# A convolution, layer norm and feed-forward kernel on one core: products moved from VectorE to GpSimd in the head, ScalarE for the first statistics, a finer tail, a new order

## The chip, the cores and the metric

The kernel runs on one core of a Trainium2 chip. The metric is the device time of one execution in microseconds; the time before is the median of three runs, 844.35 us. One execution was also taken with the hardware profiler: it took 843.82 us, and its span, from the first to the last instruction, is 842.0 us. TensorE (PE), VectorE (DVE), ScalarE (ACT) and GpSimd (POOL) work through queues of their own in order; SyncE (SP) issues most of the DMA transfers, and GpSimd issues those that add onto data in place.

## The reference

For x of shape (8, 4224, 192) and weights of shape (8, 4224, 8, 7), both float32:

```python
w = softmax(weight_gen, over the 7 taps)               # per token and head
x_pad = 6 zero tokens ahead of x                       # per batch
out[b, s, h, :] = sum_k w[b, s, h, k] * x_pad[b, s + k, h, :]     # 8 heads of 24 channels
xn = (out - mean) / sqrt(var + 1e-6) * g_ln
result = out + maximum(xn @ w_ch1, 0) @ w_ch2          # 192 -> 768 -> 192
```

The weights of the feed-forward part are given as float64.

## The kernel before

The 33,792 tokens lie on 128 partitions, 264 columns of 192 channels each; a column is one token per partition. Work goes by parts of 4, 4, then 8 and then 12 columns (`PARTS`, L22), cut into chunks of 2, 4 or 6 columns, and by groups of 4 columns (`NT`) for the matmuls.

The softmax (`softmax`, L451) makes log-weights for pieces of 4, 8 and then 12 columns: a maximum on VectorE, a subtraction on GpSimd, an exponential on ScalarE, the sum on VectorE (for two early pieces on TensorE), a logarithm on ScalarE and a second subtraction, `less`, on GpSimd. For each chunk `conv` (L492) lets ScalarE write the exponentials `wn` (key `expw`) into PSUM, and VectorE multiplies x by them: taps 1 and 2 (key `c0`), 3 and 4 (`c1`), 0 (`c2`) and 5 and 6 (`c3`), each pair into a product buffer `pr`, of which there are five. For the first three chunks (`PMUL = 3`) `c3` is GpSimd's, from a copy of the exponentials in SBUF (key `keep`). The seven products of the first three chunks are summed by TensorE (`z0` to `z3`, matmuls with the identity), whose result ScalarE copies back. In later chunks two DMA additions issued by GpSimd (`d0`, `d1`) and four additions on GpSimd (`a0` to `a3`) do it.

`norm` (L599) takes mean and variance. For parts that start below column 8 (`STATS = 8`) VectorE does it with `bn_stats` (key `stats`), two columns at a time; later ScalarE does it in two passes per column with an accumulator (`sums`, `squares`). `rstd` on ScalarE and `newton` on VectorE follow, then ScalarE normalizes (`xh`). For the first two groups TensorE transposes (`tp`) and ScalarE and VectorE split the result into two float16 halves (`thi`, `tlo`). From the third group on the split is `hi` on ScalarE and `lo` on GpSimd and the transpose is a DMA that SyncE issues (`turn`), kept apart from the DMA additions: each waits until the last one of the other kind has landed.

For each group TensorE then computes three units of the first product into the two `ph` buffers (`unit`, L780, 36 matmul pairs); ScalarE applies the relu into a float16 half (`relu`, L796) and VectorE computes the rest (`hlo`, L798), which frees `ph`. Two half passes `p0` and `p1` (L832) make the second product in the one `po` buffer, and VectorE adds it to the tokens (`f`, L884), which frees `po`; SyncE stores them. The last group's second product is made by `output` (L853): four tiles in pairs of two in one bank, one addition and one store for each pair.

Ahead of all this `weights` (L992) turns the float64 weights into scaled float16 halves on ScalarE and VectorE (keys that begin with `w_`); TensorE makes the low halves with scaled identities (`w_l`, `w_l2`), ScalarE copies them (`w_lc`, `w_lc2`).

The order of everything is written out by hand: `PLACE` (L39) gives each operation a place, operations are emitted in the order of their places, each into its engine's queue, and buffers are assigned in the same order:

```python
out = sorted(self.ops, key=lambda o: o.place)
...
b.slot = min(range(len(tenant[b.pool])), key=lambda i: freed(tenant[b.pool][i]))
```

Of the kernel before, what the change touches and what calls it, by code (L numbers as in the profile page):

```python
# [26 lines left out]
PMUL = 3  # L27
STATS = 8
# [11 lines left out]
    'wload': (0, 1, 15, 26, 98, 102, 176, 495, 321, 482, 657, 761, 837, 1034, 613, 1145, 1282, 1182, 951, 1438,  # L40
        1515, 1614, 1730,),
    'load': (2, 3, 5, 7, 9, 22, 43, 95, 105, 145, 143, 174, 92, 244, 288, 208, 297, 414, 325, 484, 497, 660,
        569, 626, 644, 719, 851, 815, 920, 942, 918, 1001, 1066, 1240, 1236, 1303, 1205, 1365, 1353, 1467, 1476,
        1619, 1541, 1592, 1669, 1749, 1853, 1832, 1814, 1980, 2003, 1949,),
    'w_load': (45, 13, 20,),
    'w_gain': (40, 38, 29,),
    'w_load2': (32,),
    'w_as': (88,),
    'w_ap': (90,),
    'w_av': (96, 99,),  # L50
    'w_an': (107,),
    'w_cs': (53,),
    'w_cp': (52,),
    'w_cv': (58, 60,),
    'w_cn': (80,),
    'w_s1': (113, 118,),
    'w_d': (150, 124,),
    'w_h': (127, 123,),
    'w_l': (155, 126,),
    'w_lc': (166, 130,),  # L60
    'w_m': (169, 172, 135, 133,),
    'w_c2s': (73, 103, 120,),
    'w_c2p': (71, 94, 125,),
    'w_c2v': (76, 79, 108, 110, 134, 138,),
    'w_c2n': (83, 116, 142,),
    'w_s2': (148, 156, 185,),
    'w_d2': (178,),
    'w_h2': (175, 164, 183,),
    'w_l2': (184, 181, 189,),
    'w_lc2': (200, 202, 194,),  # L70
    'max': (4, 11, 54, 64, 188, 281, 355, 559, 594, 537, 769, 881, 907, 1073, 1096, 1211, 1320, 1225, 1430,
        1502, 1679, 1770, 1960,),
    'sub': (6, 16, 59, 81, 193, 378, 448, 565, 599, 679, 779, 887, 972, 1091, 1124, 1261, 1400, 1415, 1513,
        1598, 1759, 1811, 2007,),
    'exp': (8, 21, 63, 111, 215, 382, 467, 592, 637, 709, 795, 903, 1023, 1105, 1148, 1276, 1412, 1459, 1581,
        1645, 1822, 1849, 2023,),
    'sum': (10, 25, 234, 390, 492, 601, 645, 721, 834, 946, 1032, 1138, 1178, 1279, 1435, 1511, 1605, 1676,
        1835, 1860, 2034,),
    'log': (12, 28, 86, 152, 249, 409, 498, 604, 658, 765, 858, 969, 1036, 1160, 1251, 1341, 1458, 1524, 1608,
        1699, 1856, 1869, 2060,),  # L80
    'less': (14, 31, 87, 160, 276, 421, 510, 606, 691, 771, 883, 987, 1058, 1193, 1257, 1344, 1478, 1559, 1650,
        1742, 1859, 1937, 2093,),
    'expw': (17, 30, 35, 56, 97, 139, 151, 199, 235, 266, 327, 356, 329, 434, 473, 516, 540, 623, 656, 703, 722,
        783, 820, 910, 960, 996, 1017, 1080, 1111, 1210, 1203, 1280, 1359, 1372, 1402, 1503, 1494, 1594, 1564,
        1678, 1721, 1775, 1796, 1888, 1944, 1972, 2058, 2145, 2102, 2104,),
    'keep': (18, 39, 65,),
# [16 lines left out]
    'copy': (50, 69, 119,),  # L103
    'stats': (61, 74, 144, 141,),
    'rstd': (77, 147, 209, 279, 354, 426, 502, 585, 693, 802, 895, 1002, 1102, 1201, 1307, 1420, 1501, 1623,
        1713, 1817, 1926, 2018, 2119, 2214, 2280, 2338,),
    'newton': (91, 153, 219, 285, 359, 432, 507, 591, 696, 804, 901, 1003, 1106, 1204, 1309, 1433, 1510, 1627,
# [10 lines left out]
    'thi': (136, 180,),  # L118
    'tlo': (159, 186,),
# [19 lines left out]
    'sums': (131, 168, 191, 187, 222, 242, 268, 258, 323, 310, 338, 334, 380, 399, 413, 411, 478, 457, 486, 490,  # L139
# [149 lines left out]
def kernel(  # L289
# [309 lines left out]
    def norm(pa):  # L599
# [3 lines left out]
        def row(i):  # L603
            if S0 < STATS:
                i = {1: 3, 2: 4}[i]
            return at(s4)[:, i, :n]
# [538 lines left out]
```

## Time and profile before

| | us |
|---|---|
| median of 3 runs | 844.35 (843.34 to 845.62) |
| profiled execution | 843.82 |
| span of it | 842.0 |
| PE busy | 821.4 (98%) |
| DVE busy | 736.5 (87%) |
| POOL busy | 701.6 (83%) |
| ACT busy | 683.8 (81%) |

The busy times are sums over the whole span. In the page's 40 slices of 21 us PE has 6, 8 and 8 tenths in the first three and 7 in the last, and 9 or more in between; DVE, ACT and POOL are at 9 tenths or near it until late and thin out in the last quarter. So the engines' shares of the whole say little about the first 60 us, which have limits of their own and are read by stretches.

### The profile page before, as it was taken

What the parts mean: (1) busy time and instruction counts of PE and PEld (TensorE: products, weight loads), DVE (VectorE), ACT (ScalarE), POOL (GpSimd) and SP (SyncE); (2) the same over time, 40 slices, a digit from 0 to 9 for tenths busy, and PEclk for the clock granted to TensorE, in tenths of its full rate; (3) what the DMA queues carried; (4) which work ended last, traced back from release to release, by engine and by line L of the source; (5) the groups of instructions that cost most, each with busy time, mean ns of one, the idle gap of its engine ahead of it and who ended that gap; (6) DMA issues with size and microseconds to landing.
All of it is one profiled execution on the core that took longest, in us unless ns stands there. A gap on an engine that the chain in (4) does not pass through costs nothing.

```text
span 842.0 us, 37407 instructions
## 1 busy us (share of the span) xinstructions
PE 821.4 (98%) x16724; PEld 811.3 (96%) x16724; DVE 736.5 (87%) x685; ACT 683.8 (81%) x1774; POOL 701.6 (83%) x402
## 2 busy tenths in 40 slices
PE   6889999999999999999999999999999999999997
PEld 5669999999999999999999999999999999999997
DVE  7999999999999999999999999999989896745332
ACT  3899998898998899898888979988888878776431
POOL 4999999999999999999999999899798879624000
PEclk9889999999999999999999999999999999999999
DMA  9997997989999997889878997777877766352432
GB/s 228 206 211 153 221 162 170 204 160 205 193 195 191 199 215 167 178 186 215 190 153 202 188 217 174 164 185 163 180 153 162 165 145 129 78 116 68 80 65 58
DMA packets 133887, 140.88 MB, mean 167 GB/s; under 512 B 104294, under 2 KB 106222, under 8 KB 133726
## 3 DMA queue, kind: packets, MB, share of 16 engines
q1 hardware_dynamic: 120190, 88.16, 45.9%
q0 software_dynamic: 13536, 50.34, 30.8%
q8 instruction: 130, 2.13, 1.0%
q14 instruction: 31, 0.25, 0.1%
HBM read 36.43 MB, written 25.95 MB: 74 GB/s over the span
## 4 chain that ended last, share of the span: by engine, by line
PE 82%; DVE 11%; issue 2%; POOL 2%; ACT 1%; DMA 1%; SPq 1%; DVEq 0%; POOLq 0%; ACTq 0%
PE po L832 41%; PE ph L780 40%; DVE pr L535 6%; DVE hlo L798 2%; DVE y L535 1%; POOL y L538 1%; DMA x<-in_x_dram 1%; PE ph L861 1%; DVE y L884 1%; POOL pr L541 1%; ACT hh L796 0%; DVE mx L466 0%; ACT junk L611 0%; DVE sm L482 0%; DVE s L628 0%
## 5 line engine op out<-in xcount | busy, mean ns | idle before, releaser
L538 POOL TENSOR_TENSOR y<-y,pr 128x1152 f32<-128x1152 f32 (+1 forms) x188 | 488.3, 2625 | 13.0 <-DVE y L535 4.3
L780 PE MATMUL ph<-xT,c_w 64*128 64x256 f16 x7128 | 412.9, 269 | 1.9 <-DVE hlo L798 1.3
L780 PEld LDWEIGHTS <-c_w 64*128 64x128 f16 x7128 | 386.2, 94 | 3.1 <-issue 2.9
L832 PE MATMUL po<-c_w2h,hh 64*128 64x192 f16 x3120 | 388.0, 243 | 1.1 <-DVE y L884 1.1
L832 PE MATMUL po<-c_w2l,hh 64*128 64x192 f16 x3120 | 388.0, 243 | 0.0
L832 PE MATMUL po<-c_w2h,hlo 64*128 64x192 f16 x3120 | 388.0, 243 | 0.0
L535 DVE TENSOR_TENSOR pr<-x,wn 128x2304 f32<-128x2304 f32 (+2 forms) x147 | 333.2, 2276 | 4.3 <-POOL y L538 2.5
L832 PEld LDWEIGHTS <-hh 64*128 64x128 f16 x6240 | 309.7, 94 | 1.4 <-issue 1.3
L798 DVE SCALAR_TENSOR_TENSOR hlo<-ph,hh 128x1024 f16<-128x1024 f32 x198 | 239.4, 1217 | 73.1 <-ACT hh L796 72.6
L796 ACT ACTIVATE hh<-ph 128x1024 f16<-128x1024 f32 x198 | 200.2, 1014 | 84.8 <-PE ph L780 80.6
L832 PEld LDWEIGHTS <-hlo 64*128 64x128 f16 x3120 | 177.6, 94 | 0.0
L758 POOL TENSOR_TENSOR hl<-xh,hl 128x768 f16<-128x768 f32 x64 | 114.7, 1828 | 49.1 <-ACT hl L756 48.3
L686 ACT ACTIVATE xh<-y,s 128x192 f32<-128x192 f32 x264 | 125.8, 536 | 17.2 <-DVE s L674 12.1
L616 ACT ACTIVATE junk<-y,s 128x192 f32<-128x192 f32 x256 | 115.8, 452 | 7.9 <-PE po L832 1.8
L541 POOL DMA_DIRECT2D pr<-pr x94 | 93.2, 1054 | 26.6 <-DVE pr L535 22.1
L611 ACT ACTIVATE junk<-y 128x192 f32<-128x192 f32 x256 | 92.1, 360 | 12.5 <-PE po L832 4.1
L884 DVE SCALAR_TENSOR_TENSOR y<-po,c_fs,y 128x768 f32<-128x768 f32 (+1 forms) x83 | 67.9, 835 | 7.4 <-PE po L832 7.2
L535 DVE TENSOR_TENSOR y<-x,wn 128x1152 f32<-128x1152 f32 (+2 forms) x50 | 59.9, 1199 | 0.0
L756 ACT ACTIVATE hl<-xh 128x768 f16<-128x768 f32 x64 | 53.4, 836 | 1.6 <-PE po L832 0.7
L611 ACT ACTIVATION_READ_ACCUMULATOR junk<-y 128x1 f32 x256 | 48.1, 188 | 0.0
L616 ACT ACTIVATION_READ_ACCUMULATOR junk<-y,s 128x1 f32 x256 | 47.9, 187 | 0.0
L486 POOL TENSOR_TENSOR e<-e,sm 128x672 f32<-128x672 f32 (+2 forms) x23 | 37.8, 1645 | 6.6 <-ACT sm L484 6.6
(86 smaller groups left out, 308.3 us busy)
## 6 DMA issues: line engine op xcount, KB each, us to landing
pr<-pr POOLq DMA_DIRECT2D x68, 576.0 KB, 6.1
x<-in_x_dram SPq DMA_DIRECT2D x34, 576.0 KB, 6.0
out_dram<-y SPq DMA_DIRECT2D x34, 576.0 KB, 4.9
pr<-pr POOLq DMA_DIRECT2D x26, 384.0 KB, 5.0
w<-in_weight_gen_dram SPq DMA_DIRECT2D x21, 336.0 KB, 5.1
x<-in_x_dram SPq DMA_DIRECT2D x14, 384.0 KB, 6.2
out_dram<-y SPq DMA_DIRECT2D x13, 384.0 KB, 5.2
x<-in_moe_w_ch_dram SPq DMA_DIRECT2D x1, 1152.0 KB, 11.3
```

Source lines behind the costliest of these rows:

```text
L535: E.tensor_tensor(out=ov, in0=xv, in1=wv, op=ALU.mult)
L538: Q.tensor_tensor(out=flat(0), in0=flat(0), in1=flat(k), op=ALU.add)
L541: return Q.dma_start(flat(to), flat(k), accum_op=ALU.add, max_dma_last_dim=CHUNK * D * 4)
L611: A.activation(junk, at(y)[:, j, :], AF.Identity, scale=-SQ / D, accum_out=at(s4)[:, 3, t : t + 1])
L616: A.activation(junk, at(y)[:, j, :], AF.Square, scale=SQ, bias=at(s4)[:, 3, t : t + 1], accum_out=at(s4)[:, 0, t : t + 1])
L686: A.activation(paired(xh, t), at(y)[:, i, :].rearrange("p (c q) -> p c q", q=P // 2), AF.Identity, bias=row(2 if quick else 3)[:, g + t : ...
L758: lambda xh=xh, hl=hl: Q.tensor_tensor(out=halves(hl, True), in0=pairs(xh), in1=halves(hl, False), op=ALU.subtract),
L780: T_.matmul(ph[:, r, v * 2 * P : (v + 1) * 2 * P], W["w1"][rows, WB[r][c], w, f : f + P], xv[rows, a, c, :, :], start=(v == 0 and k == 0), ...
L796: lambda: A.activation(at(hh)[:, us, :], at(ph), AF.Relu), [ph], [(hh, u)])
L798: lambda: V.scalar_tensor_tensor(out=at(hlo)[:, us, :], in0=at(ph), scalar=0.0, in1=at(hh)[:, us, :], op0=ALU.max, op1=ALU.subtract),
L832: made.append(T_.matmul(at(po)[:, z, e * D : (e + 1) * D], token(b, 2 * z + e, j)[rows], W[w][rows, j, :], start=(ph == 0 and e == 0 and k ...
L884: V.scalar_tensor_tensor(out=ysl, in0=at(po)[:, zs[0] : zs[-1] + 1, : 2 * D], scalar=W["fs"][:, 0:1], in1=ysl, op0=ALU.mult, op1=ALU.add)
```

## The change

`PMUL` becomes 4, and a new constant `PTWO` names column 2. GpSimd thereby makes `c3` of columns 8 to 11 and, for the chunk of columns 2 and 3, `c1` besides `c3`; the chunk of columns 8 to 11 gets a `keep` copy of its exponentials for that. `STATS` becomes a tuple with the one start 4: the statistics of columns 0 to 3 go from VectorE's `bn_stats` to ScalarE's two passes. The last four tiles go through a new function `last`: each tile into a bank of its own and with an addition of its own; columns 0 and 1 are stored together, 2 and 3 each by itself. The place list is new up to about place 480; after that each engine's order is as before, until the last tiles.

```diff
-PMUL = 3
-STATS = 8
+PMUL = 4
+STATS = (4,)
+PTWO = (2,)
...
-            if c < PMUL and i == 3:
+            if c < PMUL and (i == 3 or i == 1 and t0 in PTWO):
                 op("Pool", q_ns(2 * nd), (f"c{i}", t0), lambda k=k: mul(k, 2, Q), [*xr, (e, "w", c)], w)
...
-            if S0 < STATS:
+            if S0 in STATS:
...
-        quick = S0 < STATS
+        quick = S0 in STATS
...
+    def last(gp, t, s):
+        e = t % 2
+        if e == 0:
+            gp["po"] = Buf("ph")
+        po, ks = gp["po"], triples(gp)
+
+        def mm():
+            for k, (b, j, w) in enumerate(ks):
+                T_.matmul(at(po)[:, e, :D], token(b, t, j), W[w][:, j, :], start=k == 0, stop=k == len(ks) - 1)
+
+        op("PE", 1490, ("o", s), mm, whole(gp), [(po, e), "pe"], lat=360.0)
+        y, j = ycol(gp["pa"], gp["g"] + t)
+
+        def final():
+            V.scalar_tensor_tensor(out=at(y)[:, j, :], in0=at(po)[:, e, :D], scalar=W["fs"][:, 0:1],
+                                   in1=at(y)[:, j, :], op0=ALU.mult, op1=ALU.add)
+
+        op("V", v_ns(D, 63), ("f", s), final, [(po, e), "fs"], [(y, j)])
+        if t > 0:
+            i, n = (j, 1) if t > 1 else (j - 1, 2)
+            t0 = chunks[-1]["S"] + i
+            sp(("u", s), lambda: SY.dma_start(tokens(out, t0, n), at(y)[:, i : i + n, :].rearrange("p t d -> p (t d)")),
+               [(y, i + q) for q in range(n)], [], dma_ns(n * D * 2))
...
     for t in range(NT):
-        output(prev, t, C)
+        last(prev, t, C)
```

The place lists give these queues in the head (keys, with the chunk's first column in brackets; the weights' keys begin with `w_`):

```
SyncE before:  w 0, w 1, x 0 (two pieces), x 0 (first rows), x 2, x 4, w_load, w 2, ...
SyncE after:   w 0, x 0 (first piece), w 1, x 0 (second piece, first rows), x 2, w 2, x 4, w_load, ...
GpSimd before: sub, less, sub, less, c3[0], c3[2], sub, c3[4], d0[8], d1[8], sub, less, a0[8] to a3[8], d0[12], ...
GpSimd after:  sub, less, sub, c3[0], c1[2], less, c3[2], sub, c3[8], a0[8], a1[8], d0[8], d1[8], c3[4], less, sub, d0[12], a2[8], a3[8], ...
VectorE after: max, sum, c0[0], max, c2[0], c1[0], sum, c0[2], max, c2[2], c2[4], c0[4], w_cv, w_cv, c2[8], c1[8], c0[8], w_c2v, w_c2v, c1[4],
               w_c2v, max, newton, w_c2v, w_av, w_av, c0[12], c2[12], w_s1, c1[12], c3[12], w_c2v, stats, w_c2v, stats, c0[16], newton, tlo,
               c3[16], c2[16], w_s2, c2[20], c0[20], c1[16], tlo, c3[20], c1[20], max, w_s2, hlo, c0[24], hlo, ...
ScalarE after: exp, log, expw[0], expw[2], keep, exp, keep, log, expw[4], keep, expw[8], keep, copy, w_cp, w_cs, sums, squares, exp, copy,
               sums, w_c2p, w_c2s, squares, w_c2n, w_c2p, w_c2s, rstd, log, w_as, w_ap, w_cn, xh, w_c2n, expw[12], w_an, xh, ...
```

TensorE's order in the head is as before, but for where the copies of `w_lc2` come between its first units: the first unit now stands ahead of the copy of the last third.

## Rows read from the trace of the kernel before

**Rows 1.** Cores: span and granted clock.

```profile
core 0: 842.0 us, clock 0.994
```

**Rows 2.** TensorE's timeline at 52 to 65 us: start, length, what, idle before it.

```profile
52.72 4.19 PE L780 MATMUL ph<-xT,c_w 64*128 64x256 f16 x72 [0.58 <-ACT c_w2l L1080]
57.23 2.14 PE L780 MATMUL ph<-xT,c_w 64*128 64x256 f16 x36 [0.32 <-DVE hlo L798]
60.03 4.11 PE L780 MATMUL ph<-xT,c_w 64*128 64x256 f16 x72 [0.66 <-DVE hlo L798]
```

**Rows 3.** TensorE later: two rows of its timeline, then two of the chain.

```profile
143.41 4.11 PE L780 MATMUL ph<-xT,c_w 64*128 64x256 f16 x72
168.47 3.78 PE L780 MATMUL ph<-xT,c_w 64*128 64x256 f16 x66
...
168.65 3.93 PE ph L780 x72
819.63 3.93 PE ph L780 x72
```

**Rows 4.** Busy time by stretch: PE, PEld, DVE, ACT, POOL, granted clock, DMA share, GB/s.

```profile
10.00:20.00 10.00, 10.00 (x55) 9.87 (x54) 9.97 (x13) 3.53 (x9) 5.25 (x5) 1.00 1.06 268
20.00:30.00 10.00, 10.00 (x39) 6.92 (x38) 9.76 (x15) 7.21 (x19) 9.55 (x7) 1.00 0.90 207
40.00:50.00 10.00, 8.26 (x32) 6.12 (x32) 9.69 (x17) 9.23 (x28) 9.92 (x8) 0.67 1.00 210
```

**Rows 5.** VectorE's timeline at 125 and at 147 us.

```profile
125.36 5.02 DVE L535 TENSOR_TENSOR pr<-x,wn 128x2304 f32<-128x2304 f32 x2 [0.98 <-POOL y L538]
...
147.56 1.01 DVE L884 SCALAR_TENSOR_TENSOR y<-po,c_fs,y 128x768 f32<-128x768 f32 x1
```

**Rows 6.** VectorE's timeline in the first 28 us.

```profile
7.30 0.95 DVE L535 TENSOR_TENSOR pr<-x,wn 128x768 f32<-128x768 f32 x1 [1.58 <-DMA x<-in_x_dram]
...
9.16 2.67 DVE L535 TENSOR_TENSOR pr<-x,wn 128x768 f32<-128x768 f32 x3
...
18.23 0.56 DVE L628 BATCH_NORM_STATS2 s<-y 128x6 f32<-128x384 f32 x1
...
25.29 1.75 DVE L535 TENSOR_TENSOR pr<-x,wn 128x1536 f32<-128x1536 f32 x1
```

**Rows 7.** SyncE's queue at the start.

```profile
0.74 1.32 SPq L448 DMA_DIRECT2D w<-in_weight_gen_dram  x2
```

**Rows 8.** GpSimd's timeline at 9 to 23 us.

```profile
9.77 0.97 POOL L486 TENSOR_TENSOR e<-e,sm 128x448 f32<-128x448 f32 x1 [2.58 <-ACT sm L484]
10.69 1.55 POOL L535 TENSOR_TENSOR pr<-x,e 128x768 f32<-128x768 f32 x1
15.44 1.55 POOL L535 TENSOR_TENSOR pr<-x,e 128x768 f32<-128x768 f32 x1 [3.20 <-PE ph L560]
...
19.91 2.90 POOL L535 TENSOR_TENSOR pr<-x,e 128x1536 f32<-128x1536 f32 x1 [1.15 <-ACT e L502]
```

**Rows 9.** ScalarE's timeline: a pair of sums and squares ends where the second starts.

```profile
46.23 0.36 ACT L611 ACTIVATE junk<-y 128x192 f32<-128x192 f32 x1
...
48.23 0.60 ACT L1071 ACTIVATE c_w2h<-hlo,c_r 128x384 f16<-128x384 f32 x1
```

**Rows 10.** SyncE's queue at 163 us, and DMA issues of 160 to 168 us.

```profile
163.29 3.01 SPq L762 DMA_TRANSPOSE xT<-hl  x2
...
xT<-hl SPq DMA_TRANSPOSE x2, 3.4
```

**Rows 11.** VectorE's last additions, and DMA issues of 800 to 842 us.

```profile
820.03 1.01 DVE L884 SCALAR_TENSOR_TENSOR y<-po,c_fs,y 128x768 f32<-128x768 f32 x1
837.55 0.62 DVE L884 SCALAR_TENSOR_TENSOR y<-ph,c_fs,y 128x384 f32<-128x384 f32 x1 [2.27 <-PE ph L861]
...
out_dram<-y SPq DMA_DIRECT2D x2, 384.0 KB, 3.4
out_dram<-y SPq DMA_DIRECT2D x2, 192.0 KB, 2.5
```

More of the change, by code (lines that the diff above doesn't have):

```diff
@@ L39 @@
 PLACE = {
[L40 to L85, printed above, removed]
@@ L86 @@
-    'keep': (18, 39, 65,),
[16 rows of a table removed]
[L103 to L107, printed above, removed]
[10 rows of a table removed]
-    'thi': (136, 180,),
-    'tlo': (159, 186,),
[19 rows of a table removed]
-    'sums': (131, 168, 191, 187, 222, 242, 268, 258, 323, 310, 338, 334, 380, 399, 413, 411, 478, 457, 486, 490,
[6 rows of a table removed]
@@ L146 @@
-    'squares': (154, 173, 195, 206, 259, 247, 275, 277, 332, 346, 341, 349, 388, 401, 419, 422, 481, 468, 499,
[15 rows of a table removed]
-    'turn': (239, 282, 308, 317, 400, 410, 471, 477, 549, 554, 618, 639, 652, 727, 755, 740, 825, 848, 862, 939,
[3 rows of a table removed]
-    'halo': (316, 563, 768, 1130, 1345, 1638, 2061,),
-    'unit': (197, 203, 212, 220, 227, 243, 260, 267, 284, 302, 309, 326, 344, 351, 367, 384, 391, 406, 423, 430,
[10 rows of a table removed]
-    'relu': (204, 214, 217, 231, 236, 251, 270, 283, 296, 313, 319, 340, 358, 373, 377, 393, 404, 418, 431, 442,
[10 rows of a table removed]
@@ L189 @@
-    'hlo': (207, 216, 223, 237, 253, 261, 278, 287, 305, 318, 324, 343, 362, 379, 383, 402, 412, 420, 436, 451,
[14 rows of a table removed]
-    'hop': (246, 286, 331, 368, 407, 446, 485, 522, 555, 588, 628, 665, 699, 735, 772, 809, 844, 878, 915, 948,
[16 rows of a table removed]
+    'wload': (0, 2, 11, 34, 109, 139, 323, 497, 284, 418, 660, 764, 840, 1037, 616, 1148, 1285, 1185, 954, 1441,
+        1518, 1617, 1733,),
+    'load': (1, 3, 6, 8, 13, 22, 61, 104, 50, 146, 177, 245, 103, 150, 190, 334, 415, 442, 513, 466, 500, 663,
+        572, 629, 647, 722, 854, 818, 923, 944, 921, 1004, 1070, 1243, 1238, 1306, 1208, 1367, 1356, 1470, 1479,
+        1622, 1544, 1595, 1672, 1752, 1856, 1835, 1817, 1983, 2006, 1952,),
@@ new lines @@
+    'w_load': (31, 19, 18,),
+    'w_gain': (43, 53, 38,),
+    'w_load2': (25,),
+    'w_as': (94,),
+    'w_ap': (97,),
+    'w_av': (100, 105,),
+    'w_an': (112,),
+    'w_cs': (57,),
+    'w_cp': (56,),
+    'w_cv': (60, 64,),
+    'w_cn': (99,),
+    'w_s1': (115, 120,),
+    'w_d': (131, 124,),
+    'w_h': (138, 125,),
+    'w_l': (157, 128,),
+    'w_lc': (167, 132,),
+    'w_m': (171, 174, 136, 153,),
+    'w_c2s': (76, 87, 116,),
+    'w_c2p': (75, 85, 129,),
+    'w_c2v': (80, 81, 90, 98, 137, 143,),
@@ new lines @@
+    'w_c2n': (83, 106, 148,),
+    'w_s2': (152, 170, 208,),
+    'w_d2': (180,),
+    'w_h2': (173, 176, 179,),
+    'w_l2': (185, 182, 195,),
+    'w_lc2': (191, 193, 202,),
+    'max': (4, 20, 39, 93, 205, 307, 404, 562, 598, 540, 772, 884, 910, 1077, 1099, 1214, 1323, 1228, 1433,
+        1505, 1682, 1773, 1963,),
+    'sub': (5, 24, 52, 108, 215, 347, 472, 568, 602, 681, 782, 890, 973, 1093, 1127, 1264, 1403, 1418, 1516,
+        1601, 1762, 1814, 2010,),
+    'exp': (7, 27, 68, 127, 224, 365, 482, 595, 640, 712, 798, 906, 1026, 1108, 1151, 1279, 1415, 1462, 1584,
+        1648, 1826, 1852, 2026,),
@@ new lines @@
+    'sum': (9, 30, 232, 372, 493, 604, 648, 724, 837, 949, 1035, 1141, 1181, 1282, 1438, 1514, 1608, 1679, 1838,
+        1863, 2037,),
+    'log': (10, 35, 92, 154, 242, 377, 502, 607, 661, 768, 861, 972, 1039, 1163, 1254, 1345, 1461, 1527, 1611,
+        1702, 1859, 1872, 2063,),
+    'less': (12, 40, 101, 164, 277, 421, 510, 609, 694, 773, 885, 988, 1061, 1196, 1259, 1347, 1481, 1562, 1653,
+        1744, 1862, 1939, 2095,),
+    'expw': (14, 15, 44, 48, 110, 142, 119, 207, 218, 270, 306, 345, 362, 430, 473, 519, 543, 626, 659, 706,
+        725, 786, 823, 914, 963, 999, 1020, 1083, 1115, 1213, 1206, 1283, 1362, 1375, 1405, 1506, 1497, 1597,
+        1567, 1681, 1724, 1779, 1799, 1891, 1947, 1975, 2061, 2148, 2105, 2107,),
@@ new lines @@
+    'keep': (17, 29, 46, 49,),
[16 rows of a table added]
+    'copy': (55, 71, 122,),
+    'sums': (59, 73, 155, 144, 187, 197, 251, 240, 263, 257, 308, 324, 342, 333, 403, 390, 406, 411, 458, 486,
[7 rows of a table added]
+    'squares': (65, 78, 159, 181, 199, 210, 282, 244, 279, 271, 356, 349, 346, 339, 422, 394, 425, 414, 479,
[7 rows of a table added]
+    'rstd': (89, 151, 216, 286, 359, 428, 505, 589, 696, 805, 898, 1005, 1106, 1204, 1310, 1423, 1504, 1626,
+        1716, 1820, 1929, 2021, 2122, 2217, 2283, 2341,),
+    'newton': (95, 158, 221, 290, 364, 431, 509, 594, 699, 807, 904, 1006, 1109, 1207, 1312, 1436, 1513, 1630,
[10 rows of a table added]
@@ new lines @@
+    'thi': (134, 186,),
+    'tlo': (160, 189,),
+    'stats': (145, 141,),
[27 rows of a table added]
+    'turn': (241, 278, 319, 332, 399, 407, 460, 463, 556, 561, 619, 642, 655, 730, 758, 743, 828, 851, 865, 941,
[3 rows of a table added]
+    'halo': (292, 566, 771, 1133, 1348, 1641, 2064,),
+    'unit': (198, 203, 212, 223, 230, 246, 262, 269, 287, 303, 311, 328, 344, 351, 366, 385, 392, 408, 426, 432,
[10 rows of a table added]
+    'relu': (204, 213, 220, 233, 237, 254, 274, 289, 296, 315, 327, 338, 353, 363, 378, 397, 400, 419, 434, 441,
[10 rows of a table added]
+    'hlo': (209, 217, 225, 238, 255, 261, 280, 295, 302, 322, 343, 340, 361, 384, 380, 402, 416, 423, 438, 454,
[14 rows of a table added]
@@ L221 @@
+    'hop': (248, 291, 331, 369, 410, 450, 484, 526, 557, 592, 631, 668, 702, 738, 775, 813, 847, 881, 918, 951,
[16 rows of a table added]
 }
```

239 rows, old and new, of the table PLACE are left out of this document.

## The prediction

> **What bounds the kernel now.** I read the span and clock first, then busy time by stretch, then TensorE's own timeline, because it shows where the kernel stops being bound by one thing and starts being bound by another. The span is 842.0 us [rows 1]; the profiled execution took 843.82 us, so 1.82 us lie around the span, and it is 0.53 us under the median of 844.35 us.
>
> TensorE's stream of unit products starts at 52.72 us, waits twice for `hlo`, and has no gap after 60.03 us that is worth naming except near 130 to 150 us [rows 2]. From 168.65 us on it is saturated: 55 groups of four columns in 650.98 us, 11.836 us each [rows 3]. Nine such groups after 60.03 us would have brought it to 166.55 us; the tenth pair of units starts at 168.47 us [rows 3], so 1.92 us are lost between. After 168 us nothing but TensorE matters, until the tail. So three things can be won or lost: the head (to 60.03 us), the 1.92 us, and the tail.
>
> In the head VectorE has no free time: 9.97, 9.76 and 9.69 us busy of 10 in the stretches shown, while GpSimd has 4.75 us free in the first of them and ScalarE 6.47 and 2.79 us in the first two; by 40 to 50 us all three are full [rows 4]. The 1.92 us come from GpSimd: VectorE waited 0.98 us for an addition that frees a product buffer, then ran two long multiplies, and its final addition of 147.56 us, which frees `po`, came after TensorE wanted it [rows 5].
>
> **The change part by part, VectorE.** It loses the product of taps 3 and 4 of columns 2 and 3 (one of three that take 2.67 us, so 0.89), that of taps 5 and 6 of columns 8 to 11 (1.75, start to start 1.67) and two statistics of 0.56 (start to start 0.48) [rows 6]: 0.89 + 1.67 + 0.96 = 3.5 us. No queue is free for it at no cost, so I followed each place list in the diff engine by engine.
>
> **Start.** The first multiply waited for x until 7.30 us [rows 6]. The list now puts that load ahead of the second load of weights; two such issues take 1.32 us [rows 7], so it goes 0.66 us earlier: first multiply at about 6.65. TensorE's gathers of the first three chunks follow it and shift with it.
>
> **GpSimd.** It gains 1.55 us and 2.90 us, what the same shapes took there [rows 8]: 4.45 us. Between 9.77 and 23 us it waited 2.58, 3.20 and 1.15 us before three of its instructions [rows 8], 6.9 us, so the room is there; but what stands behind the new work in its queue waits. The first new product stands ahead of `less` of the second softmax piece: subtraction 0.97 from 8.0, two products of 1.55, `less` 0.97 [rows 8], so 13.1, and with the exponentials 13.4 for the weights of columns 4 to 7. VectorE has run out of other work at about 12.4 (6.65, eight short instructions of 0.5 to 0.9 us, and 0.45 of waiting for maxima and sums): a hole of 0.9 us. The second new product and two additions to columns 8 to 11 stand ahead of taps 5 and 6 of columns 4 to 7; these end at about 26.7, TensorE asks for them at 27.8. Later it waits about 2.4 us for VectorE's products of columns 12 to 15. Balance: 4.45 us more work, some 4.4 us less waiting, so it stands at the transposes of the third group where it stood, within 1 us (I take +0.2).
>
> **ScalarE.** Sums and squares of two columns take 48.23 - 46.23 = 2.00 us together [rows 9], so columns 0 to 3 cost 4.0 us, placed between the first copy and the weights of the second matrix, in the 6.47 + 2.79 us that were free. What hides them is that room; without it the first unit comes 4.0 us later. They make VectorE wait there twice, by my walk 0.9 us (first third of the second matrix) and 0.65 us (weights of columns 12 to 15). With 0.5 us of small gaps all VectorE holes make 0.9 + 0.9 + 0.65 + 0.5 = 2.95 us.
>
> **Head.** VectorE reaches the first `hlo` 0.65 + 3.5 - 2.95 = 1.2 us earlier, less 0.1 for the order (a maximum moved behind the first multiply, the final scale behind the transposes): 1.1. TensorE's first unit waited 0.58 us for ScalarE's copy of the last third of `c_w2l` [rows 2]; in the new list it stands ahead of that copy and takes the other `ph` buffer, but behind the matmuls of that third, which need the second transpose's `tlo` from VectorE. By the walk: 51.7, a gain of 1.0. Unit 0 to `relu` to `hlo`, one product, `hlo`, fourth unit, as before: the stream starts at 59.05 instead of 60.03. I take -1.0. Bounds: -3.5 if no hole arises, +0.5 if the holes are 1.5 us longer.
>
> **The 1.92 us.** The order up to about 140 us is new: additions of columns 40 to 43 stand ahead of two DMA issues, and the long products of columns 48 to 53 behind a short one. VectorE is 1.1 us early and the wait of 0.98 us [rows 5] has no cause left: its final addition ends 2.1 us earlier, at 148.57 - 2.1 = 146.5. TensorE wants it at about 145.8 (143.41 [rows 3] and two units of 1.97, less 1.0 of head and some 0.5 of the 1.92 that it had lost by then): 0.6 us stay. Next late would be the transpose for the group at 168.47 us: issued at 163.29, landing after 3.4 [rows 10], so 166.7; from about 145 us GpSimd's order is the old one, and it comes at 166.4 at best. So TensorE cannot be there before 166.4: 2.1 us gained in all, 1.0 of head and 1.1 of the 1.92. Bounds: 0 if GpSimd is 2 us late (then nothing of the head remains), 4 if it is 2 us early.
>
> **Tail.** Now each tile has its bank, its addition and, for the last two, its store. The last addition works on 192 columns instead of 384: 0.62 us, and 768 took 1.01 [rows 11], a slope of 0.39 per 384, so 0.43: -0.19. The last store is 96 KB instead of 192: 3.4 us for 384 KB and 2.5 for 192 [rows 11], slope 0.45 per 96 KB, so 2.05: -0.45 (0 if all that is left is fixed). The added issue of the third tile lies 1.5 us ahead of the last one, and an issue takes about 0.6, so it hides. Sum -0.64, bounds -0.2 and -0.7. The Trainium skill, DMA: Bandwidth & Descriptors, Anatomy of one DMA, gives some 2.0 us fixed plus bytes over 436 GB/s for the GpSimd path; by that the halving is worth an estimated 0.2 us, not 0.45, and the sum would be 0.2 us higher. The two rows shown have the steeper slope.
>
> **Sum.** 842.0 - 2.1 - 0.64 = 839.3 us of span, 841.1 us as a profiled execution, 841.6 us as a median.
>
> **Rivals.**
> - **GpSimd cancels the head.** Its head leaves it almost no slack once the additions begin (9.92 of 10 us [rows 4]); if its new holes are 2 us longer than I found, the transpose at 163.29 us is 2 us later and TensorE gains nothing before 168 us. Then only the tail stays: 844.35 - 0.64 = 843.7. For: that full stretch. Against: 6.9 us of waits to fill.
> - **No holes.** VectorE finds work in the order where I see it wait, and GpSimd comes early with it. Head -2.5, the 1.92 us all regained, tail -0.64: about 5 us, of which the transpose lets 3.5 pass: 840.2 and down to 839.
> - **Slower: ScalarE.** If the four columns' statistics don't fit ahead of 30 us, because the chain behind them (second matrix's words, its squares, the exponentials) is what the first unit waits for, then 4.0 us go on the head, since from 40 us ScalarE has 0.77 us of 10 free [rows 4]: 844.35 + 4.0 - 0.64 = 847.7. It decides from about 3.2 us of the 4.0 on. For: the first unit did wait for ScalarE [rows 2]. Against: 9.3 us free before 30 us.
> - **TensorE begins its stream slow.** The granted clock was 0.67 in 40 to 50 us [rows 4], between half-rate and full; the first two units took 4.19 us at full rate [rows 2]. At the lower of 1.2 and 2.4 GHz each would take 2 us more, the first `hlo` comes 2 us later: 843.6. Against: the same matmuls stand ahead of it.
> - **The tail gives nothing,** and the rest as forecast: 842.2.
>
> **How the numbers follow.** Forecast 0.46 (own range 840.3 to 842.9), GpSimd 0.21, no holes 0.17, ScalarE 0.07, slow start 0.04, tail 0.05. The range takes in all but ScalarE and the far ends: 839.0 to 845.0. 0.3% of 844.35 is 2.5 us, about what can be told from no change: faster is below 841.8. That holds for the no-holes case, a bit over half of the forecast and a little of the tail case: 0.17 + 0.29 + 0.01 = 0.47; slower (above 846.9) is ScalarE and 0.01 of GpSimd: 0.08; the same 0.45.
>
> **What would show it.** Right: first multiply at 6.6 to 6.8; the fourth unit near 59.0; VectorE holes near 12.5, 21 and 29 us; ScalarE's first sums near 16 us; no wait for `y` near 125 us; a last addition of 0.43 us and a last store that lands 0.4 us sooner; 11.84 us per group as before. Wrong: a fourth unit after 60, a wait of TensorE for `xT` near 71, 83 or 166 us, or a first unit that starts after 53 us behind ScalarE.

## The result and the profile after

The changed kernel takes 850.7 us (median of 6 runs, 849.5 to 853.3) where the kernel before took 844.4 (median of 6): a ratio of 1.008, with a 95% interval of 1.0062 to 1.0098. It is slower by 6.3 us; the forecast was 841.6. The profiled execution took 849.51 us:

```profile
core 0: 847.5 us, clock 0.996
```

The span is 5.5 us longer than that of [rows 1], at a granted clock of 0.996 against 0.994. TensorE's timeline of the changed kernel, where the stream of unit products begins:

```profile
51.18 4.10 PE L782 MATMUL ph<-xT,c_w 64*128 64x256 f16 x72
55.69 2.14 PE L782 MATMUL ph<-xT,c_w 64*128 64x256 f16 x36 [0.41 <-DVE hlo L800]
58.49 4.11 PE L782 MATMUL ph<-xT,c_w 64*128 64x256 f16 x72 [0.65 <-DVE hlo L800]
```

Against [rows 2] the fourth unit comes 1.54 us earlier; the wait for the copy of `c_w2l` is gone. So the head was won. VectorE's timeline shows the earlier start and two of the three forecast holes, near 12.5 and 29 us; the one near 21 us did not come:

```profile
6.63 0.95 DVE L537 TENSOR_TENSOR pr<-x,wn 128x768 f32<-128x768 f32 x1 [1.41 <-ACT wn L500]
...
13.52 0.95 DVE L537 TENSOR_TENSOR y<-x,wn 128x768 f32<-128x768 f32 x1 [1.01 <-ACT wn L500]
...
29.60 1.75 DVE L537 TENSOR_TENSOR pr<-x,wn 128x1536 f32<-128x1536 f32 x1 [0.88 <-ACT wn L500]
```

What was won is gone by 173 us. The chain of the changed kernel (start, length, what) goes from the landing of an addition by DMA over the landing of two transposes to TensorE:

```profile
159.91 7.92 DMA pr<-pr
167.97 5.17 DMA xT<-hl
173.19 4.10 PE ph L782 x72
```

The group that stood at 168.65 us [rows 3] stands at 173.19: 4.54 us later, and 114.70 us behind the fourth unit, where nine groups of 11.836 us make 106.52. So 8.2 us are lost on the way instead of some 2. TensorE's waits between 58 and 176 us (sum, times, longest) name the transposes; those for `xT` are 0.33, 1.07, 1.60 and 2.19 us, at 70.8, 84.1, 97.9 and 173.2 us:

```profile
PE ph L782 <- DMA xT<-hl: 5.2, 4, 2.2
PE ph L782 <- DVE hlo L800: 1.8, 4, 0.7
```

GpSimd's timeline, and under it SyncE's queue, over the same stretch (GpSimd's `pr<-pr` are the additions by DMA, `d0` and `d1`; SyncE's DMA_TRANSPOSE are the `turn`s):

```profile
63.58 2.22 POOL L760 TENSOR_TENSOR hl<-xh,hl 128x768 f16<-128x768 f32 x1
...
71.34 1.77 POOL L543 DMA_DIRECT2D pr<-pr  x2 [1.99 <-DMA xT<-hl]
...
84.61 1.77 POOL L543 DMA_DIRECT2D pr<-pr  x2 [1.27 <-DVE hlo L800]
...
142.41 1.77 POOL L543 DMA_DIRECT2D pr<-pr  x2 [1.69 <-DMA xT<-hl]
```

```profile
79.37 1.41 SPq L764 DMA_TRANSPOSE xT<-hl  x1
...
93.08 1.42 SPq L764 DMA_TRANSPOSE xT<-hl  x1
...
150.87 0.60 SPq L444 DMA_DIRECT2D x<-in_x_dram  x1
...
167.97 3.11 SPq L764 DMA_TRANSPOSE xT<-hl  x2
```

GpSimd reaches the third group's `lo` at 63.58 us, 0.8 earlier than before. Then it stands three times in front of additions by DMA, 1.99 + 1.27 + 1.69 = 4.95 us, each time until a transpose has landed. (The second is put down to `hlo`, which was long done; the transpose of 79.37 us lands after 4.7 us, at 84.1.) Before, it stood 0.32 + 0.68 us there, and for VectorE:

```profile
69.91 1.77 POOL L541 DMA_DIRECT2D pr<-pr  x2 [0.32 <-DVE pr L535]
...
121.70 1.77 POOL L541 DMA_DIRECT2D pr<-pr  x2 [0.68 <-DVE pr L535]
```

The transposes of [rows 10], issued at 163.29 us, are issued at 167.97. Of these 4.7 us, 3.5 are GpSimd's: it issues the last addition by DMA ahead of them at 159.91 us, before at 156.45. The rest is that this addition lands later.

The tail lost as well: from the first of the last four tiles to the end it takes 847.5 - 836.13 = 11.37 us, before 842.0 - 831.40 = 10.60. TensorE's timeline, then VectorE's last addition, then the DMA issues of 800 to 848 us:

```profile
838.38 0.24 PE L863 MATMUL ph<-c_w2h,hh 128*128 128x192 f16 x1 [0.59 <-DVE y L869]
...
842.02 0.24 PE L863 MATMUL ph<-c_w2h,hh 128*128 128x192 f16 x1 [0.51 <-DVE y L869]
```

```profile
843.70 0.42 DVE L869 SCALAR_TENSOR_TENSOR y<-ph,c_fs,y 128x192 f32<-128x192 f32 x1 [1.74 <-PE ph L863]
```

```profile
out_dram<-y SPq DMA_DIRECT2D x1, 192.0 KB, 2.5
out_dram<-y SPq DMA_DIRECT2D x2, 96.0 KB, 2.1
```

The addition (0.42 us) and the last store (2.1 us instead of 2.5) are as forecast. But the second tile of each `ph` buffer starts only after a wait of 0.59 and 0.51 us, when the addition of the first has read that buffer's other half.

Together: 4.54 at 173 us, 0.77 in the tail, 0.2 between.

### The profile page after: what moved, and what is told of

Same layout as the page of the kernel before. It is cut to its first block, busy times and chain, and to the rows that moved or that the text cites. A ratio compares the mean times of both kernels' runs of the same rounds, so it can differ in the third digit from the quotient of the medians.

```text
span 847.5 us, 37434 instructions
## 1 busy us (share of the span) xinstructions
PE 822.7 (97%) x16724; PEld 803.0 (95%) x16724; DVE 734.6 (87%) x683; ACT 687.2 (81%) x1791; POOL 705.8 (83%) x404
## 4 chain that ended last, share of the span: by engine, by line
PE 79%; POOL 7%; DVE 5%; issue 3%; DMA 3%; ACT 2%; SPq 1%; DVEq 0%; POOLq 0%; ACTq 0%
PE po L834 39%; PE ph L782 39%; POOL y L540 4%; DVE pr L537 2%; DVE hlo L800 2%; POOL pr L543 1%; DMA x<-in_x_dram 1%; DMA pr<-pr 1%; PE ph L863 1%; ACT xh L688 1%; DMA xT<-hl 1%; POOL e L488 1%; POOL pr L537 0%; ACT junk L618 0%; ACT hh L798 0%
## 5 line engine op out<-in xcount | busy, mean ns | idle before, releaser
L782 PEld LDWEIGHTS <-c_w 64*128 64x128 f16 x7128 | 378.6, 94 | 17.2 <-DMA xT<-hl 6.1
L834 PEld LDWEIGHTS <-hh 64*128 64x128 f16 x6240 | 305.5, 94 | 0.5
L834 PEld LDWEIGHTS <-hlo 64*128 64x128 f16 x3120 | 173.6, 94 | 0.0
L618 ACT ACTIVATE junk<-y,s 128x192 f32<-128x192 f32 x260 | 117.5, 452 | 7.7 <-PE po L834 1.5
```

The lines of the kernel that those rows point to most:

```text
L618: A.activation(junk, at(y)[:, j, :], AF.Square, scale=SQ, bias=at(s4)[:, 3, t : t + 1], accum_out=at(s4)[:, 0, t : t + 1])
L782: T_.matmul(ph[:, r, v * 2 * P : (v + 1) * 2 * P], W["w1"][rows, WB[r][c], w, f : f + P], xv[rows, a, c, :, :], start=(v == 0 and k == 0), ...
L834: made.append(T_.matmul(at(po)[:, z, e * D : (e + 1) * D], token(b, 2 * z + e, j)[rows], W[w][rows, j, :], start=(ph == 0 and e == 0 and k ...
```

## Experiments

The kernel before ran beside each of them; its median was 843.9 to 844.2 us throughout.

**Tail, and whose order.** The first four. One is this edit of `last`:

```diff
-        e = t % 2
-        if e == 0:
-            gp["po"] = Buf("ph")
+        e = 0
+        gp["po"] = Buf("ph")
```

The others join the two place lists: `a` and `b` are all operations in the changed order and in that of the kernel before.

```
e2:  [x for x in a if place(x) < 240] + the rest in the order of b    (work and tail as changed)
e3:  [x for x in b if place(x) < 239] + the rest in the order of a    (work and tail as before)
e4:  as e2, with 300 for 240
```

> The changed kernel, and nothing else of it altered than this: each of the last four tiles takes a `ph` buffer of its own instead of the second half of its neighbour's. Theory (the tail lost because the second tile of a buffer waits for the addition of the first): both waits of TensorE for `y` near the end, 0.59 and 0.51 us, and what goes with them disappear, the time from the first of the four tiles to the end of the span falls from 11.4 to about 9.9 us, and the median is 1.1 to 1.5 us under that of the changed kernel. Rival (the gap is the change of bank, not the buffer): the gaps of some 0.75 us stay and the time is within 0.3 us of the changed kernel.

> The changed kernel with its own order up to place 240 (all of the head, all of GpSimd's added work, the statistics moved to ScalarE), and behind it the order of the kernel before; the tail is the changed one. Theory A (the new order of places 240 to 480 makes GpSimd's additions by DMA wait behind transposes, and the transposes late): TensorE's fourth unit still starts near 58.5 us, its waits for `xT` between 60 and 170 us fall from 5.2 us to under 1.5, the group that stood at 173.2 us stands at 166.5 to 168, and the median is 843 to 844.5 us (the head's gain of 1.5 less the tail's loss of 0.8 below the kernel before). Theory B (the 4.45 us of work that GpSimd took over leave it late, whatever order follows): the waits for `xT` stay above 4 us and the median stays at 849 to 851 us.

> The kernel before with its own head (its order up to place 239, its division of the work, its statistics, its tail), and behind that the order of the changed kernel. Theory A: the loss of the stretch from 60 to 170 us comes with the order alone, so TensorE waits 4 to 6 us for `xT` there and the median is 848.5 to 851 us. Theory B: without the 4.45 us of added work GpSimd has the room, the waits for `xT` stay under 1.5 us and the median is 843.5 to 845.5 us.

> As the one with the new head alone, but the changed kernel's order is kept up to place 300 (so the two additions by DMA that it puts between the first transpose and the next pair stay), and the order of the kernel before follows from there. If that first alternation is what costs, as the wait of 2.7 us for `xT` between 80 and 100 us lets one think, GpSimd stands 1.3 to 2 us near 84 us, and the median is 845.5 to 847.5 us, 2 to 3 above the kernel with the new head alone. If the loss is made further back, it is within 0.7 us of that kernel. Theory B would again give 849 to 851 us.

Measured: 849.0 us (7 runs, spread from 844.9 to 851.6; the profiled execution was the shortest), 844.3, 850.4 and 850.8. In the first, the waits for `y` are gone; VectorE's additions follow every 1.40 to 1.49 us, and the tail takes 842.8 - 832.83 = 9.97 us:

```profile
837.50 0.42 DVE L868 SCALAR_TENSOR_TENSOR y<-ph,c_fs,y 128x192 f32<-128x192 f32 x1 [1.07 <-PE ph L862]
838.99 0.42 DVE L868 SCALAR_TENSOR_TENSOR y<-ph,c_fs,y 128x192 f32<-128x192 f32 x1 [1.07 <-PE ph L862]
```

That is 0.63 under the 10.60 of before: the forecast -0.64, once the wait is out. Theory B falls: the added work of GpSimd stands in e2, which has no loss, and is missing in e3, which has all of it. The order from place 240 on makes the loss. The fourth, for which 845.5 to 847.5 was expected, I first read as proof that the loss sits between places 240 and 300. It isn't: at that seam the joined order issues two loads of weights and two of x within 2.5 us behind the second transpose, and the two additions by DMA beside them land after 12.3 us (the DMA issues of 76 to 98 us):

```profile
pr<-pr POOLq DMA_DIRECT2D x2, 384.0 KB, 12.3
```

That is a loss of its own, made by the seam. That the loads beside them make the additions so late is likely, but no run moves these four loads alone.

**The alternation.** An addition by DMA waits for the last transpose to land, and a transpose for the last addition. Up to place 570 the changed order goes from one to the other 11 times, the old one 9 times. I took that for the cause. In e5, from e2, the `d1` of columns 28 to 31 goes behind the second transpose (place 285); in e6, from e4, it goes ahead of it (280), and two others move with it. The entries of the place lists are

```diff
-    'd1': (214, 266, 259, 348,
+    'd1': (214, 265, 286, 348,
```

```diff
-    'd1': (214, 253, 294, 348,
+    'd1': (214, 253, 273, 348,
-    'd0': (219, 256, 297, 364,
+    'd0': (219, 256, 322, 364,
-    'c1': (200, 243, 285, 305,
+    'c1': (200, 243, 268, 304,
```

where only the third number of each is a move (the others count on). e7 is e2 with the tail of e1; e8 is the changed order with the three moves of e6 and the tail of e1.

> The kernel with the new head alone (844.3 us), with a single instruction put elsewhere: the addition by DMA of tap 4 to tap 3 of columns 28 to 31 (`d1`) is issued behind the second transposing DMA (`turn` 1) instead of ahead of it, as the changed kernel has it, so that additions and transposes alternate once more. Theory A, narrowed to this alternation (an addition by DMA waits for the last transpose to land, and the next transposes for the addition): the pair of transposes behind it is issued 5 to 10 us later than the 85.5 us of that kernel, and the median is 848 to 851 us. Rival (the loss of the changed order comes from other moves between places 240 and 300, VectorE's products among them): within 1 us of 844.3.

> The kernel that keeps the changed order up to place 300 (850.8 us), with three instructions put elsewhere: the same `d1` ahead of the second transpose again, VectorE's product that it needs a little earlier, and the addition of columns 32 to 35 (`d0`) behind the fourth transpose. All else that the changed kernel moved up to place 300 stays. Theory A narrowed: the alternation is gone, so the loss is: 843.5 to 845.5 us, TensorE's waits of 60 to 170 us under 2.5 us. Rival: 849 to 851 us.

> The kernel with the new head alone (844.3 us) and, at the tail, a `ph` buffer for each tile. The two edits do not touch each other, so the tail's 1.4 us come off: 842.9 us, between 842.4 and 843.4, which is 1.1 us under the kernel before: 0.75 from GpSimd being earlier by so much at 63 us and for the rest of the way, 0.6 from the tail.

> The changed kernel with its whole order, the three instructions put elsewhere as in the mended one that keeps the order up to place 300, and a `ph` buffer for each of the last tiles. Theory A narrowed (one alternation made the loss): 842.5 to 844.5 us. If the changed order loses further on as well (its additions of columns 48 to 53 stand behind the transposes of places 460 and 463): 845 to 848 us.

Measured: 845.4, 853.6, 843.1 and 850.0 us. One more alternation costs some 1.0 us, near what can be told apart, not four to seven; putting the additions back restores nothing (the moved product also makes TensorE wait 1.8 us for `y` near 76 us, a price of the edit itself). The narrowed theory fell. e7 does what was expected: 843.1, a ratio of 0.9992 (0.9983 to 1.0001), no measurable gain over the kernel before.

**One queue at a time.** Each engine has its own queue, so one queue can be taken from one order and the rest from the other, where dependencies and buffers allow it. All have the changed head and tail.

```
f1:  e2, with SyncE's queue in the changed order (transposes and additions alternate as before)
f2:  e2, with GpSimd's queue in the changed order (they alternate as in the changed kernel)
f3:  VectorE, GpSimd and ScalarE in the changed order, SyncE in the old one
f4:  VectorE and GpSimd in the changed order, ScalarE and SyncE in the old one
```

> The kernel with the new head alone (844.3 us), of whose five queues one, SyncE's, has behind place 240 the changed kernel's order; it holds the loads, the stores and the transposing DMAs, and the transposes stand in the same order among themselves and against the additions by DMA. Theory C (the changed order puts loads of weights of 336 KB between the transposes, and the transposes and additions land later beside them): 847 to 851 us. Theory A (the order of GpSimd's queue, which makes additions and transposes alternate): within 0.7 us of 844.3.

> The same with GpSimd's queue in the changed order instead, and all other queues in the order of the kernel before; with it come the two additional changes between additions by DMA and transposes. Theory A: 846.5 to 851 us, the second pair of transposes issued 4 to 8 us later than 85.5 us. Theory C: within 1 us of 844.3 (the single addition that was put behind one transpose cost 1.0 us).

> The complement: the changed order on VectorE, GpSimd and ScalarE, and the order of the kernel before on SyncE. Theory C: 843.5 to 845.5 us, since the loads stand where they stood. Theory A: 848 to 851 us as the changed kernel, whose order of additions and transposes it has.

> The changed order on GpSimd and VectorE alone. Theory A: 847 to 851 us; and if it is above the one with GpSimd's order alone by over 1 us, VectorE's order (the product that the late addition needs stands 20 places further back) has a part in it. Theory C: 843.5 to 845.5 us.

Measured: 852.8, 854.1, 844.4 and 869.5 us. f3 decides: the whole changed order but for SyncE's queue has no loss (ratio 1.0005, 0.9995 to 1.0015), with all eleven alternations in it; its runs lie in two groups, eight at 843.0 to 844.6 us and four at 846.1 to 846.8. So theory A falls and the loss comes with SyncE's queue. f2 and f4 were badly conceived: queues that were ordered for each other are torn apart, and the engines wait for one another. In f4 GpSimd's waits (58 to 200 us) are

```profile
POOL pr L548 <- DVE pr L542: 17.3, 3, 7.3
```

which says nothing on A or C. Part of f1 is of that kind too, as VectorE waits for a buffer whose store is late:

```profile
DVE y L542 <- DMA out_dram<-y: 4.1, 1, 4.1
```

**What in SyncE's queue.** The changed order issues the load of columns 66 to 71 (576 KB) at 150.87 us, just ahead of the last additions by DMA before the transposes of 168 us; the kernel before issues it near 90 us. DMA issues of 145 to 165 us (KB each, median us to landing), first in the changed kernel, then in f3:

```profile
pr<-pr POOLq DMA_DIRECT2D x3, 576.0 KB, 7.9
x<-in_x_dram SPq DMA_DIRECT2D x2, 576.0 KB, 8.7
```

```profile
pr<-pr POOLq DMA_DIRECT2D x3, 576.0 KB, 6.2
...
x<-in_x_dram SPq DMA_DIRECT2D x1, 576.0 KB, 6.6
```

All four below have the tail of e1; the first, second and fourth start from the changed kernel. g2 puts all `load` and `wload` at their old places, with `turn` and `u` at the changed ones; g5 puts all `u`, the stores, at the old ones and leaves the rest. g1 and g4 (from e7) move the load of columns 66 to 71 alone, the first to the front, the second to the back:

```diff
-    'load': (415, 442, 513, 466, 500,
+    'load': (416, 443, 337, 467, 501,
```

```diff
-    'load': (300, 417, 328, 487, 500,
+    'load': (300, 416, 512, 486, 499,
```

> The changed kernel with a `ph` buffer for each of the last tiles (849.0 us) and one instruction elsewhere: SyncE's load of columns 66 to 71 (576 KB) is issued behind that of columns 48 to 53, near 97 us, instead of near 150 us. Theory C1 (that load makes the last additions before the transposes of 163 us land late): the additions land in under 7 us, the transposes are issued 1.5 to 3 us earlier, and the median is 845.5 to 847.5 us, 1.5 to 3.5 lower. Rival C2 (the other loads, or the stores, which stand between the transposes of 66 to 96 us): within 1 us of 849.0.

> The same kernel with all loads of x and weights back where the kernel before issues them (as far as they can be among stores and transposes, whose places stay). Theory C (loads beside transposes and additions): 843 to 845 us, 4 to 6 below 849.0, as with all of SyncE's old order (844.4, less 1.4 of the tail). If the stores that stand ahead of transposes are what costs: 847.5 to 850 us.

> The kernel with the new head and a buffer for each of the last tiles (843.1 us), in which nothing but the load of columns 66 to 71 is moved: from about 90 us to the changed kernel's place near 150 us. Theory C1: the additions ahead of the transposes of 162 us land 1.5 us or more later, TensorE waits for `xT` near 167 us, and the median is 844.5 to 846.5 us. Rival C2: within 0.7 us of 843.1.

> The changed kernel with a buffer for each of the last tiles (849.0 us) and the stores of the output back where the kernel before issues them, behind the transposes; the loads stay in the changed order. Theory C: within 1 us of 849.0. If the stores cost: 844 to 847 us.

Measured: 846.8, 846.7, 843.3 and 847.1 us, against 849.0 for e1 and 843.1 for e7. In the changed order the medians fall by 2.2 us with the one load, by 2.3 with all loads and by 1.9 with the stores. With e1's seven runs spread over 6.7 us, none of the three differences is clear of the spread, and which of them is the largest can't be told. In the order of e7 the late load costs nothing that can be measured, though the additions land after 7.5 us there: TensorE does not wait for what follows from them. No single part gives back what SyncE's whole old order does (5.6 us). In g1's profile, taken in the shortest of its twelve runs, the additions of 145 to 165 us land after 6.2 us (8.0 in e1's, also its shortest), and GpSimd has a single wait between 58 and 176 us:

```profile
69.71 1.77 POOL L548 DMA_DIRECT2D pr<-pr  x2 [0.34 <-issue]
```

g1's times fall into two groups with nothing between, 842.1 to 843.3 (4 runs) and 846.4 to 848.8 (8 runs). The last two ask why, and try the best combination. g3 is f3 with the tail of e1; h1 is g1 with the load of columns 32 to 35, which stood directly behind the first transpose (place 241), moved up:

```diff
-    'load': (146, 177, 245, 103, 150,
+    'load': (146, 177, 191, 103, 150,
```

> The changed kernel with a `ph` buffer for each of the last tiles, the load of columns 66 to 71 near 97 us, and one instruction more elsewhere: the load of columns 32 to 35 is issued some 20 us earlier instead of directly behind the first transposing DMA at 66 us. If that load makes this transpose land late (5.0 instead of 3.3 us), the upper group of times goes: all runs at 842 to 844 us, median 842.8. Rival (something else decides how long the transpose takes): two groups as before, near 843 and near 847 us.

> The changed order on VectorE, GpSimd and ScalarE with the order of the kernel before on SyncE (844.4 us) and a `ph` buffer for each of the last tiles: 1.4 us less, 843.0 us, in two groups near 842.0 and near 845.0; if the two edits add up, this is the best of the kernels with the changed order, 1 us under the kernel before.

Measured: 847.8 us, all five runs at 846.0 to 848.1, and 843.4 (842.3 to 844.9). The theory falls: with no load behind it, the first transpose still lands late. Of the rival's two groups only the upper shows in these five runs; g3's two groups did not come either. SyncE's queue in h1, and then the line on landing for that transpose in h1 and in g1:

```profile
45.72 1.90 SPq L449 DMA_DIRECT2D x<-in_x_dram  x3
65.81 1.54 SPq L769 DMA_TRANSPOSE xT<-hl  x1
72.34 0.64 SPq L922 DMA_DIRECT2D out_dram<-y  x1
```

```profile
DMA to landing us min/median/max: 4.9/4.9/4.9
```

```profile
DMA to landing us min/median/max: 3.3/3.3/3.3
```

g3's ratio is 0.9996 (0.9987 to 1.0005). No version of the changed kernel beats the one before by what can be measured.

## Why the prediction was wrong

**The step that failed** is that on the 1.92 us: "the transpose for the group at 168.47 us ... from about 145 us GpSimd's order is the old one, and it comes at 166.4 at best". The place was right in part. I had that transpose issued at 163.0 us (166.4 less the landing of 3.4); it was issued at 167.97 and landed after 5.17 us, and TensorE waited 2.19 us for it. But 3.0 us more had gone in waits for three earlier transposes, of which the sum had nothing. I costed what the new order does to VectorE, and of GpSimd only its own work; the waits that the order makes between DMAs I put at nothing, without having worked them out: an addition by DMA waits for a transpose to land, a transpose for the additions. GpSimd, which has no time to spare from 60 to 150 us, stood 4.95 us in front of additions by DMA until a transpose had landed (before: 1.00 us, for VectorE), and the additions of 145 to 165 us landed after 7.9 us (before: 6.8). The queues past which steps are moved I had followed in the head alone.

Five kernels with a buffer for each of the last tiles show how far the issue of that pair of transposes goes with the time:

```
kernel   GpSimd stood, 60 to 150 us   transposes issued   TensorE waited for them   span     span less issue
g1       0.34                         161.58              0                         840.1    678.5
e7       0.49 + 0.57                  162.75              0                         840.8    678.1
g3       1.87                         163.39              0                         841.8    678.4
e1       0.37 + 1.85                  164.66              2.24                      842.8    678.1
h1       1.90 + 2.24 + 0.53 + 1.62    167.35              0                         846.2    678.9
```

With the four other such kernels (e8, g2, g4, g5) the last column reaches from 677.5 to 678.9. So the issue tells the time to within 1.4 us, but it does not set it in each of them. TensorE waited for this pair in e1 and in the changed kernel; in g1, e7, g3 and h1 it was busy up to that group, and what it had lost, it had lost ahead of it: in g3 1.60 us at 96.8 us, in h1 0.23 at 70.7 and 2.05 at 85.0, in e7 1.00 at 83.5, in g1 nothing for `xT`. TensorE's waits for `xT` between 58 and 176 us in e1, g3 and h1:

```profile
PE ph L782 <- DMA xT<-hl: 2.2, 1, 2.2
```

```profile
PE ph L787 <- DMA xT<-hl: 1.6, 1, 1.6
```

```profile
PE ph L787 <- DMA xT<-hl: 2.3, 2, 2.0
```

That GpSimd's standing makes both late, the issue and TensorE, fits the table, but is argued, as no run changes it alone.

That SyncE's queue makes the difference is shown (f3 and g3 against the changed kernel and e1: 6.3 and 5.6 us). That it does so by late landings is not: between e1 and g1, which differ in one load, the additions of 145 to 165 us land after 8.0 and 6.2 us, but the 2.2 us between the medians are not clear of the spread, and in g4 they land after 7.5 us at no cost. For the rest it is argued.

**The tail** failed by an omission: -0.64 was the right sum for the addition and the store (0.63 with a buffer for each tile, e1), but between two tiles of one buffer a wait was added, 0.59 and 0.51 us, which makes two gaps of some 0.7 us, 1.4 in all. I had written that each tile "has its bank" and not asked what orders a write to one bank behind a read of the other; what does, no run shows, only that separate buffers end it. By the fit that the Trainium skill, DMA: Bandwidth & Descriptors, Anatomy of one DMA, gives for the GpSimd path, the halved store would land an estimated 0.2 us sooner; these stores, which SyncE issues, show 2.5 and 2.1 us, 0.4 less, as the steeper slope of [rows 11] said.

**Right:** the head's mechanism: the first multiply at 6.63 (6.65 forecast), holes at 13.5 and 29.6 us, ScalarE's first sums at 15.95 us, the fourth unit at 58.49 (59.05), GpSimd 0.8 us earlier at 63.58 (0.2 later forecast, within 1). The fourth unit came 0.56 us sooner than forecast, and the hole near 21 us is missing. No wait for `y` is left near 125 us, but VectorE waits 0.47, 1.21 and 1.31 us for it at 75, 88 and 107 us. Of the head's 1.5 us little arrives: e2 with its tail mended (e7) is 0.8 us under the kernel before, of which 0.6 are the tail's. This resembles the first rival, GpSimd full, without the longer holes that it asked for: GpSimd is 1.0 us earlier at the third group's `lo` (63.36 us), and the transposes of 163.29 us come 0.5 us earlier, at 162.75.

**What would have shown it wrong** was named, waits for `xT` near 71, 83 and 166 us: they came at 70.8, 84.1 and 173.2, and one more at 97.9. The chance of 0.08 for slower rested on ScalarE but for 0.01 of GpSimd; no rival had a transfer that comes late because of others.

**Open** is which of SyncE's stores and loads do it, as no part alone gives back more than 2.3 us and loads and stores were not put back together, and why the times of g1 fall into two groups. In the traces the first transpose landed after 3.3 to 3.5 us, or after 4.8 to 5.2 with GpSimd standing 1.9 to 2.0 us behind it (4.54 in e3); what decides between them is not known. The load behind it does not (h1), nor does SyncE's new order alone: in f3 and g3, with the old one, it landed after 4.8 us. Nor was the data slow. In h1's trace all but two of this transfer's 1568 packets move between 67 and 69 us, as all of them do in g1's, and the last two start only at 69.5 us.

Two executions of one order can differ by nearly as much as the change. The profiled execution of e1 has the changed kernel's order; in it the first two transposes landed after 3.3 and 3.2 us instead of 5.0 and 4.7, GpSimd stood 2.22 us instead of 4.95, and the group of 173.19 us stood at 169.89, 3.3 us earlier. So of the 4.54 us, some 3 differ between two executions of one order, and a single trace of each kernel can't tell the order's share. That SyncE's queue makes the difference rests on medians, not on single traces.

## What to carry to other kernels

Where a place list is searched anew, the loads and stores that it moves are part of the change, even if nothing waits for them: lay the DMA queues side by side through the whole stretch in which the order differs, and ask of each transfer that others wait for what is in flight beside it. Find the events for which the engine that bounds the kernel waits (here the landings of transposes, for TensorE) and cost a change by what it does to each of them; one event that goes with the time need not be the one that sets it. Queues ordered for each other can't be mixed freely to see which is at fault: taking all but one from the new order told something, taking one or two cost 9 to 25 us. Where a kernel's times spread over several us, take more runs before parts of the difference are shared out.

## What the runs showed that was not expected

A transposing DMA of the same shape landed after 3.3 us in some executions and after 4.9 in others, in one of these (h1) with no other transfer issued from SyncE between 47.6 and 72.3 us; its last two packets came late, not its data. A write of TensorE to one half of a two-bank buffer waited in this program for VectorE's read of the other half, 0.5 to 0.6 us each time; with two buffers it didn't wait.
